# Chunk attention and two feed-forward layers on one core: where the scores of a group stand on TensorE, and in which array quadrants and banks

## The chip, the core and the metric

The kernel runs on one core of a Trainium2 chip. A core has TensorE (PE in the profile, PEld its weight loads), VectorE (DVE), ScalarE (ACT), GpSimd (POOL) and SyncE (SP), which here issues all the loads and stores. The metric is the device time of one execution in microseconds; lower is better.

## What is computed

Attention within chunks of 64 tokens (8 batches, 8 heads, 576 tokens, 64 features of a head), then two feed-forward layers over 4608 tokens of 512 features with 2048 hidden ones:

```python
def _attn_ref(q, k, v):            # chunk = 64, scale = 1 / sqrt(64)
    scores = scale * np.matmul(q_c, k_c.transpose(0, 1, 2, 4, 3))
    scores = scores - np.max(scores, axis=-1, keepdims=True)
    attn = np.exp(scores)
    attn = attn / (np.sum(attn, axis=-1, keepdims=True) + 1e-09)
    out = np.matmul(attn, v_c)

def _moe_ref(x, w_in, w_out):
    h = x @ w_in
    g = h * (1.0 / (1.0 + np.exp(-1.702 * h)))
    return g @ w_out

def _moe2_ref(x, w_in, w_out, alpha):
    h = x @ w_in
    g = np.maximum(h, 0.0) + alpha * np.minimum(h, 0.0)
    return g @ w_out
```

The weights come as 64-bit numbers and are decoded on the chip.

## The kernel before, in words

**Slots.** The first layer is a hand-written loop over 144 slots, n = 0 to 143: nine blocks of 512 tokens, in each of them the 16 slices of 128 hidden features. A slot issues on TensorE the 12 products H(n) (tile psH, line 454) and then the 12 products Y(n-2) (tile psY, line 476). ScalarE applies the activation to psH (line 461) and copies the result to the rounded part of gs (line 121); VectorE, in block 0 GpSimd, takes the rest (line 124). Two banks hold psH, four hold psY, two are left for the attention. At the end of a block psY is copied out (lines 487, 489), and the next block's x is split (`split_x`, lines 432 and 434). The second layer follows with other code; it is not changed.

**Engines keep the order of the program text.** The whole kernel is under one manual schedule: each engine, and SP's queue, takes its instructions in the order in which the Python code issues them. What fixes the order of the attention is the dictionary `between`, which hangs functions on half slots. An even place 2n is `middle` of slot n: behind the activation of H(n), ahead of the copy to gs and ahead of the decoding of weights. An odd place 2n+1 is the end of slot n, behind Y(n-2) and ahead of the slot's weight loads and preparation steps.

**Groups.** Attention goes by 36 groups g of 128 tokens (two chunks, all eight heads). Groups 0 to 3 and the scores of group 4 are done ahead of the loop, by the list `FIRST`. Group g from 5 on has its base at half slot 8(g-4), four slots a group, and goes through these steps:

- `att_T`, base-4: transposes q and k to qT and kT; by TensorE for groups up to 5 (line 318), by one VectorE instruction each from group 6 on (line 325).
- `att_S`, base-1: scores (psS, line 341), 16 float32 products of 64x64x64, each of which shows as two instructions in the trace. Product (head pair, chunk c, head j) reads rows j of the array and writes partitions j, all in one bank. Then VectorE's maximum (line 350) and subtraction (line 355) into e.
- `att_E`, base-1, directly behind: exponential on ScalarE (line 362), sum, addition and reciprocal on VectorE (lines 364 to 366), product on GpSimd (line 367). The exponential and the activation of h need different function tables, so a table load stands ahead of either when they change.
- `att_AT`, base+2: transposes e to `at`; for groups up to 7 by four TensorE transposes (line 383) and a ScalarE copy (line 388), from group 8 on by 16 VectorE transposes of 32x128 (line 393).
- `att_PV`, base+5: the sums (psX, line 410), again 16 products of 64x64x64, but product (head pair, c, j) reads rows c and writes partitions j of bank c. Two ScalarE copies (line 418) put them into x.
- `load_v` of the next group at base+6, and the q and k loads of the group after next in eight parts from base-1 to base+6 (line 300).

In block 0 each slot also decodes two slices of weights on VectorE (lines 156 to 171), which ScalarE and GpSimd then split (lines 121, 124). Slots 18 to 122 prepare the second layer's weights in 32 steps, each with such a decode whose first step on ScalarE (line 153) waits for its load.

A tile for psT, psS, psAT or half of psX is taken from the pool `ps_a`, two banks in turn, by `psum_att`.

Of the kernel before, what the change touches and what calls it, by code (L numbers as in the profile page):

```python
# [9 lines left out]
F32 = mybir.dt.float32  # L10
# [7 lines left out]
SQ = 32  # L18
# [31 lines left out]
def tile_chunk_attention_two_ffn(  # L50
# [45 lines left out]
    PS = bass.MemoryType.PSUM  # L96
    ps_y = banks.enter_context(tc.tile_pool(name="ps_y", bufs=4, space=PS, reuse_waits="tile"))
    ps_h = banks.enter_context(tc.tile_pool(name="ps_h", bufs=2, space=PS, reuse_waits="tile"))
    ps_a = banks.enter_context(tc.tile_pool(name="ps_a", bufs=2, space=PS, reuse_waits="tile"))

    ident = const.tile([P, P], F32, name="ident")
    alpha_sb = const.tile([P, NF], F32, name="alpha_sb")
# [8 lines left out]
    def psum_att(name):  # L111

        if ps_turn:
            pool, tag = ps_turn[0]
            ps_turn.append(ps_turn.pop(0))
            return pool.tile([P, 512], F32, tag=tag, name=name)
        return ps_a.tile([P, 512], F32, tag="a", name=name)

    def split(src, hi, lo, eng_hi, eng_lo):
        if eng_hi is nc.scalar:  # L120
# [236 lines left out]
        )  # L357
        e_t[g] = e

    def att_E(g):  # L360
        e = e_t[g]
        nc.scalar.activation(out=e, in_=e, func=AF.Exp, scale=SCALE)
        d = st_p.tile([P, 2 * HP, 1], F32, tag="d", name="d")
        nc.vector.reduce_sum(d, e, axis=AX.X)
        nc.vector.tensor_scalar_add(d, d, 1e-9)
        nc.vector.reciprocal(d, d)  # L366
        nc.gpsimd.tensor_tensor(  # L367
            out=e, in0=e, in1=d.to_broadcast([P, 2 * HP, CH]), op=ALU.mult
        )

    at_t = {}

    def att_AT(g):
        e = e_t.pop(g)
        if g < GPB:
            t = spare(f"wi{NF - GPB - 1 - g % 2}", 1).rearrange("p (h t) -> p h t", h=HP)
        else:
            t = at_p.tile([P, HP, P], F32, tag="at", name="at")

        if g < 2 * GPB:  # L380
            ps = psum_att("psAT")
            for hp in range(HP):
                nc.tensor.transpose(
                    ps[:, hp * P:(hp + 1) * P],
                    e[:, 2 * hp:2 * hp + 2, :].rearrange("p u t -> p (u t)"),
                    ident,
                )
            nc.scalar.copy(t.rearrange("p h t -> p (h t)"), ps)
        else:
            blocks = e.rearrange("p (h c) (b e) -> p h c b e", c=2, e=SQ)  # L390
            for i in range(P // SQ):
                for o in range(P // SQ):
                    nc.vector.transpose(  # L393
                        t[o * SQ:(o + 1) * SQ, :, i * SQ:(i + 1) * SQ],
                        blocks[i * SQ:(i + 1) * SQ, :, o // 2, o % 2, :],
                    )
        at_t[g] = t

    x_t = {}
# [1 line left out]
    def att_PV(g):  # L401
        at, vt = at_t.pop(g), qkv.pop((g, "v"))
        blk, i = divmod(g, GPB)
        if i == 0:
            x_t[blk] = x_p.tile([P, KT, NB], F32, tag="x", name="x")
        ps = [psum_att("psX") for _ in range(2)]
        for hp in range(HP):
            for c in range(2):
                for j in range(2):
                    nc.tensor.matmul(  # L410
                        ps[c][j * CH:(j + 1) * CH, hp * CH:(hp + 1) * CH],
                        vt[c * CH:(c + 1) * CH, 2 * hp + j, :],
                        at[c * CH:(c + 1) * CH, hp, j * CH:(j + 1) * CH],
                        start=True,
                        stop=True,
                    )
        for c in range(2):
            nc.scalar.copy(
                x_t[blk][:, :, i * P + c * CH:i * P + (c + 1) * CH],
                ps[c][:, :HP * CH].rearrange("p (h t) -> p h t", h=HP),  # L420
            )


    xs_t = {}
# [449 lines left out]
    with tc.manual_schedule():  # L874
# [28 lines left out]
            steps[step[:-1]](int(step[-1]))  # L903
        x_t.pop(0)
        ps_turn.clear()


        todo = {}
# [24 lines left out]

        between = {}
        for g in range(GPB, NG):
            for at, fn in zip((-4, -1, -1, 2, 5), (att_T, att_S, att_E, att_AT, att_PV)):
                if g > GPB or at > 0:
                    between.setdefault(8 * (g - GPB) + at, []).append((fn, g))
            if g + 1 < NG:
# [89 lines left out]
```

## Time and profile before

| | |
|---|---|
| median of 3 runs | 1633.4 us (1631.62 to 1634.8) |
| the profiled execution | 1633.03 us, of which 1631.1 us are the span of the profile |
| granted TensorE clock, mean | 0.993 of full |
| TensorE busy | 1586.6 us, 97% |
| weight loads | 1332.8 us, 82% |
| VectorE busy | 1121.7 us, 69% |
| ScalarE busy | 836.2 us, 51% |
| GpSimd busy | 487.6 us, 30% |
| attention products in the slots, psS / psX | 36.7 us / 23.3 us, 1024 instructions each |

All times count from the start of the span. Busy shares are means over stages with different limits, so the stretches are read one by one. In a row of the order of time the first number is the start and the second the length, both in us; an `xN` merges N instructions of one kind that stand behind each other, and the bracket at the end is the idle time of the engine just before, with what ended it.

### The profile page before, as it was taken

The page shows a single profiled execution, that of the slowest core. Times are in us where ns is not written, and L with a number is a line of the kernel's source. Part 1 is how long each engine was busy: PE and PEld are TensorE (multiplying, and loading weights), DVE is VectorE, ACT ScalarE, POOL GpSimd, SP SyncE. Part 2 cuts the span into 40 slices and gives each one's busy share as a digit, 9 for nine tenths or more (in the row PEclk, how much of TensorE's full clock was granted, in tenths as well). Part 3 has the DMA queues.
Part 4 walks back from the last instruction along what each step waited for, and adds up shares of the span by engine and source line. Part 5 has one row for each costly group of instructions (what it writes and reads, how often), then busy time and mean ns, then how long its engine had stood idle before and what let it go on. Part 6 is the DMA issues. An engine that isn't in the chain of part 4 may idle for free.

```text
span 1631.1 us, 25435 instructions
## 1 busy us (share of the span) xinstructions
PE 1586.6 (97%) x9257; PEld 1332.8 (82%) x9259; DVE 1121.7 (69%) x1634; ACT 836.2 (51%) x1198; POOL 487.6 (30%) x382
## 2 busy tenths in 40 slices
PE   6988999999999999999999999999999999999997
PEld 4766888888888888888888778888888888999997
DVE  7999566566566657657532267886788688778767
ACT  5555354444444544445433465566565556656653
POOL 3554122223132222222220034423523342342330
PEclk9999999999999999999999999999999999999999
DMA  9741444544453544444230457669767966997974
GB/s 243 209 133 22 97 114 110 128 111 123 107 137 95 141 121 111 121 121 131 68 136 0 169 171 244 199 188 245 249 190 206 269 197 211 227 343 244 257 262 124
DMA packets 384044, 268.07 MB, mean 164 GB/s; under 512 B 264112, under 2 KB 321968, under 8 KB 383920
## 3 DMA queue, kind: packets, MB, share of 16 engines
q1 hardware_dynamic: 383920, 266.46, 57.6%
q8 instruction: 73, 1.20, 0.3%
q14 instruction: 51, 0.42, 0.1%
HBM read 218.11 MB, written 48.23 MB: 163 GB/s over the span
## 4 chain that ended last, share of the span: by engine, by line
PE 88%; DVE 5%; DMA 2%; SPq 2%; issue 2%; ACT 1%; POOL 0%; DVEq 0%; POOLq 0%
PE psH L454 22%; PE psY L476 22%; PE psYa L773 12%; PE psHa L655 11%; PE psYb L773 9%; PE psHb L655 8%; PE psS L341 2%; DVE u L166 1%; PE psX L410 1%; SPq L277 1%; DVE u L156 1%; DVE u L171 1%; DMA wi2t<-wi 1%; DMA k<-in_k_dram 1%; DVE o L720 0%
## 5 line engine op out<-in xcount | busy, mean ns | idle before, releaser
L454 PE MATMUL psH<-xs,wi 128*128 128x512 f32 x1728 | 426.1, 397 | 5.2 <-DVE xs L123 5.2
L476 PE MATMUL psY<-gs,wo 128*128 128x512 f32 x1728 | 416.5, 391 | 0.0
L454 PEld LDWEIGHTS psH<-xs,wi 128*128 128x128 f32 x1728 | 322.0, 189 | 75.2 <-DVE xs L123 5.7
L476 PEld LDWEIGHTS psY<-gs,wo 128*128 128x128 f32 x1728 | 326.1, 189 | 67.8
L124 DVE TENSOR_TENSOR gs<-g,gs 128x512 fp32r<-128x512 f32 x129 | 95.2, 738 | 179.6 <-ACT gs L121 178.7
L773 PE MATMUL psYa<-o,w 128*128 128x512 f32 (+1 forms) x960 | 212.3, 369 | 4.8 <-DVE o L720 2.5
L655 PE MATMUL psHa<-xop,wi2t 128*128 128x512 f32 (+1 forms) x960 | 211.5, 369 | 3.0 <-DVE g L701 1.7
L773 PEld LDWEIGHTS psYa<-o,w 128*128 128x128 f32 x960 | 174.9, 188 | 29.8 <-DVE o L720 4.5
L655 PEld LDWEIGHTS psHa<-xop,wi2t 128*128 128x128 f32 x960 | 175.1, 188 | 27.6 <-DVE g L701 2.5
L461 ACT ACTIVATE g<-psH 128x512 f32<-128x512 f32 x144 | 86.2, 598 | 209.8 <-PE psH L454 209.0
L773 PE MATMUL psYb<-o,w 128*128 128x512 f32 (+1 forms) x720 | 158.4, 368 | 0.7 <-ACT o L715 0.7
L655 PE MATMUL psHb<-xop,wi2t 128*128 128x512 f32 (+1 forms) x720 | 158.3, 368 | 0.5 <-DVE g L701 0.5
L725 POOL TENSOR_TENSOR tsum<-g,tsum 128x1024 f32<-128x1024 f32 (+1 forms) x39 | 99.9, 2561 | 162.2 <-DVE o L720 162.2
L725 POOL TENSOR_TENSOR tsum<-g,g 128x1024 f32<-128x1024 f32 (+1 forms) x19 | 42.8, 2252 | 350.2 <-DVE g L678 344.5
L773 PEld LDWEIGHTS psYb<-o,w 128*128 128x128 f32 x720 | 131.3, 188 | 18.4 <-ACT o L715 1.3
L655 PEld LDWEIGHTS psHb<-xop,wi2t 128*128 128x128 f32 x720 | 131.4, 188 | 18.3 <-DVE g L701 0.9
L670 ACT ACTIVATE neg<-g 128x1024 f32<-128x1024 f32 (+1 forms) x80 | 78.1, 976 | 128.6 <-DVE g L701 128.0
L393 DVE STREAM_TRANSPOSE at<-e 32x128 f32<-32x128 f32 x448 | 135.5, 302 | 6.7
L367 POOL TENSOR_TENSOR e<-e,d 128x512 f32<-128x512 f32 x32 | 33.5, 1047 | 319.9 <-DVE d L366 275.5
L678 DVE SCALAR_TENSOR_TENSOR g<-g,neg 128x1024 f32<-128x1024 f32 (+1 forms) x80 | 104.5, 1306 | 19.4 <-ACT neg L672 19.4
L672 ACT ACTIVATE neg<-neg,minus_alpha 128x512 f32<-128x512 f32 (+1 forms) x160 | 100.2, 674 | 2.6
L720 DVE TENSOR_TENSOR o<-g,o 128x1024 fp32r<-128x1024 f32 (+1 forms) x60 | 96.3, 1605 | 5.5 <-ACT o L715 5.5
(111 smaller groups left out, 1828.5 us busy)
## 6 DMA issues: line engine op xcount, KB each, us to landing
wi2t<-wi SPq DMA_DIRECT2D x280, 256.0 KB, 3.7
w<-wo SPq DMA_DIRECT2D x140, 512.0 KB, 4.0
x<-ysb SPq DMA_DIRECT2D x36, 256.0 KB, 2.5
raw<-in_moe_w_in_dram SPq DMA_DIRECT2D x16, 512.0 KB, 5.1
raw<-in_moe_w_out_dram SPq DMA_DIRECT2D x16, 512.0 KB, 4.1
raw<-in_moe_w_in_dram SPq DMA_DIRECT2D x32, 256.0 KB, 3.9
wi<-stb SPq DMA_DIRECT2D x16, 512.0 KB, 3.0
raw<-in_moe_w_out_dram SPq DMA_DIRECT2D x32, 256.0 KB, 3.8
```

What stands on the lines that cost most here:

```text
L124: eng_lo.tensor_tensor(out=lo, in0=src, in1=hi.bitcast(F32), op=ALU.subtract)
L393: nc.vector.transpose(t[o * SQ:(o + 1) * SQ, :, i * SQ:(i + 1) * SQ], blocks[i * SQ:(i + 1) * SQ, :, o // 2, o % 2, :],)
L454: nc.tensor.matmul(ps, w[:, a, c], xs[:, b, c], start=(i == 0), stop=(i == 3 * KT - 1))
L461: nc.scalar.activation(out=g, in_=ps, func=AF.Gelu_apprx_sigmoid)
L476: nc.tensor.matmul(y_t[j][t], w[:, a, t * P:(t + 1) * P], gs[:, b], start=(f == 0 and a + b == 0), stop=(f == NF - 1 and b == 1),)
L655: nc.tensor.matmul(ps, w[:, c, a], x[b][:, c], start=(k == 0 and i in (1, 2, 5)), stop=(k == 5 and i in (2, 3, 4)), skip_group_check=True,)
L670: nc.scalar.activation(out=neg, in_=src, func=AF.Relu, scale=-1.0)
L672: nc.scalar.activation(out=neg[:, jj], in_=neg[:, jj], func=AF.Copy, scale=minus_alpha[:, f + jj:f + jj + 1])
L678: nc.vector.scalar_tensor_tensor(out=g, in0=g, scalar=0.0, in1=neg, op0=ALU.max, op1=ALU.add)
L720: nc.vector.tensor_tensor(out=lo, in0=wide(homes[nm], n), in1=hi.bitcast(F32), op=ALU.subtract)
L725: eng.tensor_tensor(out=wide(homes[out], n), in0=wide(homes[x], n), in1=wide(homes[y], n), op=ALU.subtract,)
L773: nc.tensor.matmul(ps[:, d, :n], w[:, jj, d, a], x[b][:, jj], start=(k == 0 and i in (1, 5, 2)), stop=(k == 5 and i in (3, 2, 4)), skip_gr ...
```

## The change

- The pool `ps_a` is closed behind the groups ahead of the loop. In its place one tile of two banks, `both[0]`, lives through the rest of the first layer. `psum_att` returns its two banks in turn, and `att_PV` writes the first half of either bank.
- `att_S` is no longer called in the slots. `att_PV(g)` issues the scores of group g+1 (`att_S_matmuls`) directly behind its own products, ahead of the ScalarE copies. They go into the second half of the banks: product (head pair, c, j) reads rows j, writes partitions c, in bank j. Maximum and subtraction (`att_S_max`) stand behind the copies. So the scores of group g stand at base-3, where they stood at base-1.
- `att_T` goes from base-4 to base-5, the exponential (`att_X`) from base-1 to base-2, which is the middle of a slot; sum, reciprocal and division (`att_N`) stay at base-1.
- e now has the chunk in the partitions. So `att_AT` of groups 5 to 7 becomes 16 float32 products with the identity of 64x64 each, and from group 8 on 8 VectorE transposes of 32x256 in place of 16 of 32x128.

```diff
+    att_banks = ExitStack()
+    ps_a = att_banks.enter_context(tc.tile_pool(name="ps_a", bufs=2, space=PS, reuse_waits="tile"))
+    both, ps_pair = [], []
@@ psum_att
-        return ps_a.tile([P, 512], F32, tag="a", name=name)
+        ps_pair.append(ps_pair.pop(0))
+        return ps_pair[0]
@@
+    def att_S_matmuls(g):
+        qt, kt = qkT.pop((g, "q")), qkT.pop((g, "k"))
+        s_t[g] = s4 = both[0][:, :, HP * CH:].rearrange("p j (h t) -> p h j t", h=HP)
+        for hp in range(HP):
+            for c in range(2):
+                for j in range(2):
+                    r = slice(j * CH, (j + 1) * CH)
+                    nc.tensor.matmul(
+                        s4[c * CH:(c + 1) * CH, hp, j, :],
+                        qt[r, hp, c * CH:(c + 1) * CH],
+                        kt[r, hp, c * CH:(c + 1) * CH],
+                        start=True,
+                        stop=True,
+                    )
+    def att_S_max(g):
+        s4 = s_t.pop(g)
+        m = st_p.tile([P, HP, 2, 1], F32, tag="m", name="m")
+        nc.vector.reduce_max(m, s4, axis=AX.X)
+        e = e_p.tile([P, 2 * HP, CH], F32, tag="e", name="e")
+        nc.vector.tensor_tensor(
+            out=e.rearrange("p (h j) t -> p h j t", j=2), in0=s4,
+            in1=m.to_broadcast([P, HP, 2, CH]), op=ALU.subtract,
+        )
+        e_t[g] = e
@@ att_AT
-        if g < 2 * GPB:
+        if g > GPB:
+            if g < 2 * GPB:
+                ps = psum_att("psAT")
+                for u in range(2 * HP):
+                    for c in range(2):
+                        r = slice(c * CH, (c + 1) * CH)
+                        nc.tensor.matmul(
+                            ps[r, u * CH:(u + 1) * CH], e[r, u, :], ident[r, r], start=True, stop=True
+                        )
+                nc.scalar.copy(t.rearrange("p h t -> p (h t)"), ps)
+            else:
+                t3 = t.rearrange("p h (j t) -> p (h j) t", j=2)
+                for i in range(P // SQ):
+                    for b in range(CH // SQ):
+                        o = i // 2 * 2 + b
+                        nc.vector.transpose(
+                            t3[o * SQ:(o + 1) * SQ, :, i % 2 * SQ:(i % 2 + 1) * SQ],
+                            e[i * SQ:(i + 1) * SQ, :, b * SQ:(b + 1) * SQ],
+                        )
@@ att_PV
-        ps = [psum_att("psX") for _ in range(2)]
+        if ps_pair:
+            ps = [both[0][:, c] for c in range(2)]
+        else:
+            ps = [psum_att("psX") for _ in range(2)]
...
+        if ps_pair and g + 1 < NG:
+            att_S_matmuls(g + 1)
         for c in range(2):
             nc.scalar.copy(
...
+        if ps_pair and g + 1 < NG:
+            att_S_max(g + 1)
@@ behind the steps of FIRST
+        att_banks.close()
+        ps_b = banks.enter_context(tc.tile_pool(name="ps_b", bufs=1, space=PS))
+        both.append(ps_b.tile([P, 2, 512], F32, tag="aa", name="psX"))
+        ps_pair += [both[0][:, c] for c in range(2)]
@@
-            for at, fn in zip((-4, -1, -1, 2, 5), (att_T, att_S, att_E, att_AT, att_PV)):
+            for at, fn in zip((-5, -2, -1, 2, 5), (att_T, att_X, att_N, att_AT, att_PV)):
```

## Rows read from the trace of the kernel before

**Rows 1.** Busy time by stretch: stretch, length; PE, PEld, DVE, ACT, POOL; clock.

```profile
99.00:138.00 39.00, 27.49 (x169) 22.21 (x169) 37.40 (x50) 21.51 (x36) 19.71 (x15) 0.89 0.24 54
...
444.00:540.00 96.00, 96.00 (x656) 78.04 (x652) 60.90 (x136) 45.20 (x71) 24.82 (x34) 1.00 0.45 116
```

**Rows 2.** TensorE in order of time: start, length, line, tiles, shape, count.

```profile
378.20 2.88 PE L476 MATMUL psY<-gs,wo 128*128 128x512 f32 x12
...
383.64 2.88 PE L476 MATMUL psY<-gs,wo 128*128 128x512 f32 x12
386.45 0.69 PE L410 MATMUL psX<-at,v 64*64 64x64 f32 x32
...
389.93 2.88 PE L476 MATMUL psY<-gs,wo 128*128 128x512 f32 x12
392.74 1.15 PE L341 MATMUL psS<-kT,qT 64*64 64x64 f32 x32
...
396.68 2.88 PE L476 MATMUL psY<-gs,wo 128*128 128x512 f32 x12
```

**Rows 3.** TensorE ahead of the loop: scores, then sums of another group.

```profile
28.41 1.08 PE L341 MATMUL psS<-kT,qT 64*64 64x64 f32 x29 [0.83 <-ACT kT L323]
...
29.38 0.64 PE L410 MATMUL psX<-early 64*64 64x64 f32 x30
```

**Rows 4.** VectorE in block 0, in order of time.

```profile
86.56 0.66 DVE L325 STREAM_TRANSPOSE kT<-k 128x512 f32<-128x512 f32 x1
...
102.40 0.69 DVE L364 TENSOR_REDUCE d<-e 128x8 f32<-128x512 f32 x1 [0.70 <-ACT e L362]
...
149.46 0.66 DVE L325 STREAM_TRANSPOSE kT<-k 128x512 f32<-128x512 f32 x1
...
155.30 3.17 DVE L434 TENSOR_TENSOR xs<-x,xs 128x512 fp32r<-128x512 f32 x4 [0.54 <-ACT xs L432]
```

**Rows 5.** TensorE in block 0, in order of time.

```profile
82.93 0.69 PE L410 MATMUL psX<-at,v 64*64 64x64 f32 x32
...
104.77 1.12 PE L383 MATMUL psAT<-ident,e 128*128 128x128 f32 x4 [6.01 <-POOL e L367]
...
137.16 1.11 PE L383 MATMUL psAT<-ident,e 128*128 128x128 f32 x4 [5.74 <-POOL e L367]
137.93 3.94 PE L476 MATMUL psY<-gs,wo 128*128 128x512 f32 x12
...
147.25 0.69 PE L410 MATMUL psX<-at,v 64*64 64x64 f32 x32
...
157.34 3.02 PE L454 MATMUL psH<-xs,wi 128*128 128x512 f32 x12
```

**Rows 6.** Group 33 at the start of a block: VectorE and TensorE.

```profile
740.27 5.08 DVE L393 STREAM_TRANSPOSE at<-e 32x128 f32<-32x128 f32 x16
...
745.25 0.83 PE L410 MATMUL psX<-at,v 64*64 64x64 f32 x32
...
746.62 0.67 DVE L325 STREAM_TRANSPOSE kT<-k 128x512 f32<-128x512 f32 x1
```

**Rows 7.** Loads of k for group 26, its transposition, landing times in 555 to 575.

```profile
562.55 1.99 SPq L300 DMA_DIRECT2D k<-in_k_dram  x4
...
572.99 0.70 DVE L325 STREAM_TRANSPOSE qT<-q 128x512 f32<-128x512 f32 x1
...
DMA to landing us min/median/max: 1.7/1.9/3.5
```

**Rows 8.** ScalarE behind a weight load, and the sums that it copies.

```profile
362.53 0.69 PE L410 MATMUL psX<-at,v 64*64 64x64 f32 x32
...
366.53 0.67 ACT L153 ACTIVATE u<-raw 128x512 f32<-128x512 f32 x1 [5.36 <-DMA raw<-in_moe_w_in_dram]
367.10 0.62 ACT L418 COPY x<-psX 128x256 f32<-128x256 f32 x2
...
368.90 1.28 ACT L362 ACT_TABLE_LOAD   x1
```

More of the change, by code (lines that the diff above doesn't have):

```diff
@@ L98, in tile_chunk_attention_two_ffn @@
     ps_h = banks.enter_context(tc.tile_pool(name="ps_h", bufs=2, space=PS, reuse_waits="tile"))
-    ps_a = banks.enter_context(tc.tile_pool(name="ps_a", bufs=2, space=PS, reuse_waits="tile"))
+    att_banks = ExitStack()
+    ps_a = att_banks.enter_context(tc.tile_pool(name="ps_a", bufs=2, space=PS, reuse_waits="tile"))
+    both, ps_pair = [], []
     ident = const.tile([P, P], F32, name="ident")
@@ L358, in att_S, with att_X, att_N @@
         e_t[g] = e
-    def att_E(g):
+    s_t = {}
+    def att_S_matmuls(g):
[22 more added lines that the diff above has]
+        e_t[g] = e
+    def att_X(g):
+        nc.scalar.activation(out=e_t[g], in_=e_t[g], func=AF.Exp, scale=SCALE)
+    def att_N(g):
         e = e_t[g]
-        nc.scalar.activation(out=e, in_=e, func=AF.Exp, scale=SCALE)
         d = st_p.tile([P, 2 * HP, 1], F32, tag="d", name="d")
@@ L369, in att_E @@
         )
+    def att_E(g):
+        att_X(g)
+        att_N(g)
     at_t = {}
@@ L388, in att_AT @@
             nc.scalar.copy(t.rearrange("p h t -> p (h t)"), ps)
[L389 to L396, printed above, removed]
         at_t[g] = t
@@ L405, in att_PV @@
             x_t[blk] = x_p.tile([P, KT, NB], F32, tag="x", name="x")
-        ps = [psum_att("psX") for _ in range(2)]
+        if ps_pair:
+            ps = [both[0][:, c] for c in range(2)]
+        else:
+            ps = [psum_att("psX") for _ in range(2)]
         for hp in range(HP):
```

## The prediction, made before the change was run

> **What bounds the kernel now.** I read the busy shares of stretches first, then TensorE's order of time, then the waits of the other engines. The reader is to see two stages inside the first layer. In block 0 (slots 0 to 15, up to about 157 us) VectorE decodes weights without a pause: from 99 to 138 us it is busy 37.40 of 39 us and TensorE only 27.49 [rows 1]. In the seven blocks after that TensorE is busy 96.00 of 96 us at full granted clock and VectorE 60.90 [rows 1]. So in block 0 a shorter TensorE step is worth nothing unless VectorE's chain gets shorter too, while from slot 16 on each TensorE microsecond that goes comes off the end. The second layer is not touched.
>
> **What one group costs TensorE.** Take the starts of psY [rows 2]. A plain slot (H, then Y) lasts 383.64 - 378.20 = 5.44 us. A slot that also holds the sums (psX) lasts 389.93 - 383.64 = 6.29, so the sums cost 0.85. A slot that holds the scores (psS) lasts 396.68 - 389.93 = 6.75, so the scores cost 1.31. Both are 32 instructions; the scores take 1.15 from first start to last end and the sums 0.69 [rows 2]. The scores of before use two quadrants, hence 16 rounds of two; the sums use four, hence 8 rounds of four. The difference of 8 rounds is 0.46 us, so 8 rounds cost 0.46.
>
> **Scores in four quadrants behind the sums.** New cost of the scores: their own 8 rounds, 0.46 us, with no entry and no exit of their own, since the sums before them have paid for both. That two different tiles follow each other without a seam is shown early in the trace, where scores started at 28.41 and the sums of another group came right behind: alone the scores end at 28.41 + 1.15 = 29.56, the sums ended at 29.38 + 0.64 = 30.02, 0.46 later [rows 3]. Each group saves 1.31 - 0.46 = 0.85. Bounds: the sums' pace is the fastest row there is for such matmuls, so 0.46 is the lower end; the upper end is the pace of two quadrants, 0.92, which leaves 0.39. I take 0.46, because the new scores go through the same four quadrants and the same two banks as the sums. Groups 9 to 35 lie in the stage that TensorE bounds: 27 x 0.85 = 22.9 us.
>
> **Block 0, groups 5 to 8.** VectorE's queue sets the pace here. Its sum of exponentials waited 0.70 us for ScalarE's exponential directly behind the subtraction [rows 4], in groups 5, 6 and 7 alike. With the subtraction a slot earlier the exponential is long done, so VectorE's chain gets 3 x 0.70 = 2.1 us shorter, and the transposition of group 7's probabilities, which waited 5.74 us for GpSimd's division, starts at 137.16 - 2.1 = 135.1 [rows 5]. Against that stands the earlier place of the scores. They now need qT and kT when the sums end, and in block 0 VectorE delivers these late: for group 6 the sums start at 82.93 and kT ends at 86.56 + 0.66 = 87.2; for group 8 it is 147.25 against 149.46 + 0.66 = 150.1 [rows 4, 5]. So TensorE waits at the scores of groups 6 and 7 for 4 to 5 us, and arrives at the transpositions about 1 us early instead of 6: the wait moves, it isn't added. What group 5's own steps win or lose at the start of the block, with four slots of VectorE's queue still ahead, ends in the 6.01 us wait of group 6 [rows 5]. Exit of the block: transposition of group 7 in its new form (16 products in two quadrants, priced like the old scores, 1.31) from 135.1 to 136.4; Y to 139.2, at full clock instead of the 3.94 us after the long wait [rows 5]; H and Y to 144.6; sums to 145.3; the scores of group 8 wait for kT until 150.1 - 2.1 = 148.0 and end at 148.6; H and two Y (8.3) bring slot 16 to 156.9, against 157.34 before [rows 5]: 0.4 us gained. Bounds: VectorE's split of x, which ended at 155.30 + 3.17 = 158.5 [rows 4], comes only 2.1 - 1.4 = 0.7 earlier, since the maximum and subtraction of group 8 now stand before it; H needs it after two thirds of its 2.9 us, so at most 1.4 is gained. On the other side the 2.7 us wait may lower the clock again; the rows put that at 1.1 (3.94 against a plain 2.88 [rows 2, 5]) and I allow twice as much, so at most about 1.8 is lost.
>
> **VectorE in the other blocks.** Transpositions of q and k move half a slot ahead and scores a whole one, so the cover between them shrinks from one and a half slots to one. In the tightest group, 33, kT ends at 747.29 while the sums start at 745.25 and end their share 0.6 later: 1.4 us late [rows 6]. What takes that away: 8 transpositions in place of 16. One of 32x128 takes 5.08 / 16 = 0.32 and one with four times the columns 0.67 [rows 6]; between them, an estimate of 0.44 for double the columns, 8 x 0.44 = 3.5 instead of 5.08, 1.5 us less in front of q and k. Also the maximum and subtraction (1.4 us) no longer stand in that stretch's queue. I leave 0.3 us for this one group; the six other groups at a block's start were late by under 1.0 and get the same relief, and the rest were ready in time.
>
> **Edits at no cost, and their cover.** The q and k loads keep their places on SP's queue, ahead of the value load as before. Transpositions come 2.7 us earlier; the shortest distance from the last k issue to the transposition is 572.99 - 564.54 = 8.4 us, landing takes at most 3.5 [rows 7], so 2.2 us are left. The exponential now stands between the activation of h and its split: one table load, 1.28 us [rows 8], and 0.6 of work, with the copy to gs behind it. That gs is read two slots later, some 11 us. The number of table loads stays. GpSimd's division keeps its place; its input is ready earlier.
>
> The lasting pair adds an order: sums and scores share both banks, so ScalarE's copies of the sums wait for the scores (0.46 later) and VectorE's maximum waits for the copies (0.62 more). Behind the copies stands the next activation, which waits for H, 2.9 us later; behind the maximum the prep's decode and the next split. The Trainium skill, "PSUM — Partial Sum Buffer", section Terms, speaks against sharing: two engines at one bank and quadrant at once are an error, reads against reads included. No run here shows that; by it the order can't be dropped, and rival (d) below keeps its mechanism; without it (d) would have no chance at all.
>
> **Sum.** 22.9 + 0.4 - 0.3 = 23.0 us. The profiled execution took 1633.03 us (span 1631.1), 0.4 under the median of three, 1633.4. That gives 1610.0 by the profiled one; I forecast 1610.
>
> **Rivals.**
> (a) The scores stand waiting for kT at each block's start, because the shorter transposition doesn't help as much as I think. Price: the 1.4 us of rows 6, seven times, 10 us: 1620. For it: TensorE itself gets 3.5% faster, which VectorE must follow. Against: VectorE has 35% to spare there [rows 1]. 9%.
> (b) Four quadrants run at the pace of two because the order of rows differs from the sums'. 27 x 0.39 = 10.5 us: 1622. Against: old scores alternated the same way. 5%.
> (c) Each small matmul has a floor of issue, so that 32 scores cost more than 8 rounds. Bounded by rows 2 between 0.46 and 0.92, at the middle 27 x 0.62 = 16.7: 1616. The Trainium skill, "TensorEngine Tiling (Array Packing)", section Performance Considerations, Instruction Overhead, states about 60 cycles for each matmul; an estimate by that page at 2.4 GHz is 32 x 25 ns = 0.8 us, or 1619. The sums' 32 within 0.69 us, the last one's own length included, say no [rows 2]. 3%.
> (d) Slower. Where ScalarE sits behind a weight load, as from 362.5 on, the sums' copies come at 367.10, 4.6 us after the sums' start [rows 8]. VectorE's maximum now waits for them, and its queue with it. Should this use up the distance from a split to the product that reads it (about two slots), TensorE waits some 4.6 us and loses 1.1 of clock, 5.7 a time. Four groups had such late copies (rows 8 stand for them), and 4 x 5.7 = 22.8 would eat the gain; from the fifth on the kernel is slower than before, and with six it stands at 1610 + 34 = 1644. Against: the decode behind the maximum waits for that same load anyway. 5%.
> (e) Block 0 gives more than 1.4 us: 1606 to 1608. 3%.
>
> **Chances.** Forecast (1606 to 1614) 75%, rivals as above. The range runs from 1606 to 1620: block 0 by its bounds (-1.4 to +1.8), the noise of the runs (1631.62 to 1634.8), and rivals (a) and (c); left out are (b) and (d). A measurement here tells 0.2% (3.3 us) from no change: faster 0.92, same 0.03, slower 0.05.
>
> **What would show it.** Right: psX and psS as one block of 64 in about 1.15 us; four slots with a group in 23.1 instead of 23.9 us; psY starts at full clock, no TensorE waits after slot 16; 8 transpositions in about 3.5 us; the sum of exponentials without its 0.70. Waits at psS for VectorE in groups 6 to 8, and short ones at psAT. Wrong: a seam or a gap inside psX and psS, waits at psS in later blocks, psY waiting for gs, or VectorE idle at the maximum with a queue behind it.

## The result, and the profile after

The changed kernel takes 1605.85 us (median; 1604.85 to 1607.76), the kernel before 1632.51 (median of 4; 1630.86 to 1634.8): a ratio of 0.9837, 95% interval 0.982 to 0.9854. The profiled execution took 1604.85 us, with a span of 1603.1 where before's was 1631.1. The time lies below the forecast of 1610 and just under the range, which began at 1606.

The 28.0 us of span lie here. H of slot 16, the end of block 0, starts at 152.61 in place of 157.34: 4.7 us. The seven blocks from there to the last one take 645.9 us in place of 668.7: 22.8 us. The last block takes 89.76 both times, and the second layer, whose code is the same, 0.5 less, which is not the change's. The forecast had 22.9 - 0.3 for the groups of the later blocks and 0.4 for block 0. So the term on which it rested came out, and block 0 gave more than the bound that I had put on it (1.4).

TensorE in order of time, after, around group 30 (start, length, line, tiles, shape, count):

```profile
671.25 2.88 PE L532 MATMUL psY<-gs,wo 128*128 128x512 f32 x12
674.06 0.69 PE L462 MATMUL psX<-at,v 64*64 64x64 f32 x32
674.57 0.65 PE L373 MATMUL psX<-kT,qT 64*64 64x64 f32 x32
675.15 3.02 PE L510 MATMUL psH<-xs,wi 128*128 128x512 f32 x12
678.01 2.88 PE L532 MATMUL psY<-gs,wo 128*128 128x512 f32 x12
```

The scores (line 373, named psX now since they share its tile) begin 0.51 us behind the first of the sums and end 1.16 behind it; the next H starts 1.09 behind the sums' start. The slot lasts 678.01 - 671.25 = 6.76 us, so sums and scores cost 6.76 - 5.44 = 1.32 together, where they cost 0.85 + 1.31 = 2.16 before [rows 2]. That is the 0.84 that the forecast put at 0.85, and four slots with a group last 23.08 us.

ScalarE and VectorE, after, behind the same products:

```profile
675.29 0.65 ACT L472 COPY x<-psX 128x256 f32<-128x256 f32 x2 [2.59 <-PE psX L373]
675.97 0.69 DVE L384 TENSOR_REDUCE m<-psX 128x8 f32<-128x512 f32 x1 [2.54 <-ACT x L472]
...
681.90 0.68 DVE L398 TENSOR_REDUCE d<-e 128x8 f32<-128x512 f32 x1
```

The order through the shared banks is there as foretold: the copies wait for the scores, the maximum for the copies. The sum of exponentials has no wait any more, where it had 0.70 [rows 4]. Over the whole kernel the maximum waits 69.4 us in 27 waits, and none of it reaches TensorE.

Busy time in the two stretches of [rows 1], after (us; PE, PEld, DVE, ACT, POOL, granted clock, DMA share, GB/s):

```profile
99.00:138.00 39.00, 33.18 (x250) 27.09 (x250) 38.86 (x49) 21.68 (x37) 23.54 (x18) 0.91 0.31 77
444.00:540.00 96.00, 96.00 (x685) 78.89 (x676) 57.45 (x107) 45.94 (x75) 25.43 (x34) 1.00 0.48 124
```

The later blocks are still TensorE's alone, at full clock. In block 0 VectorE is now busy 38.86 of 39 us; the wait for the exponential is gone from its queue, and TensorE is busy 5.7 us more in that stretch than before.

TensorE in block 0, after; a bracket is the idle time just before, with what ended it:

```profile
82.63 0.69 PE L462 MATMUL psX<-at,v 64*64 64x64 f32 x32
84.51 0.69 PE L373 MATMUL psX<-kT,qT 64*64 64x64 f32 x32 [1.19 <-DVE kT L328]
...
100.15 1.15 PE L424 MATMUL psX<-ident,e 64*64 64x64 f32 x32 [1.12 <-POOL e L401]
...
115.04 1.13 PE L373 MATMUL psX<-kT,qT 64*64 64x64 f32 x32 [4.70 <-DVE kT L328]
116.10 4.34 PE L510 MATMUL psH<-xs,wi 128*128 128x512 f32 x12
...
131.25 1.15 PE L424 MATMUL psX<-ident,e 64*64 64x64 f32 x32
...
143.65 0.69 PE L373 MATMUL psX<-kT,qT 64*64 64x64 f32 x32 [2.24 <-DVE kT L328]
144.27 3.06 PE L510 MATMUL psH<-xs,wi 128*128 128x512 f32 x12
...
152.61 2.88 PE L510 MATMUL psH<-xs,wi 128*128 128x512 f32 x12
```

The waits of 6.01 and 5.74 us at the transpositions of the probabilities [rows 5] are gone or 1.12 long, and three waits for kT stand at the scores. But everything is earlier than the forecast had it: the transposition for group 7 at 131.25 and not 135.1, the scores of group 8 at 143.65 and not 148.0.

### The profile page after: what moved, and what is told of

Its sections match the earlier page's. It is cut to its first block, busy times and chain, and to the rows that moved or that the text cites. A ratio compares the mean times of both kernels' runs of the same rounds, so it can differ in the third digit from the quotient of the medians.

```text
span 1603.1 us, 25410 instructions
## 1 busy us (share of the span) xinstructions
PE 1560.8 (97%) x9341; PEld 1318.4 (82%) x9343; DVE 1080.9 (67%) x1410; ACT 832.8 (52%) x1198; POOL 491.3 (31%) x382
## 4 chain that ended last, share of the span: by engine, by line
PE 88%; DVE 6%; issue 2%; SPq 1%; DMA 1%; ACT 1%; POOL 0%; DVEq 0%; POOLq 0%; ACTq 0%
PE psH L510 23%; PE psY L532 22%; PE psYa L829 12%; PE psHa L711 12%; PE psYb L829 9%; PE psHb L711 8%; DVE u L169 2%; PE psX L462 1%; DVE u L159 1%; SPq L280 1%; DVE u L174 1%; PE psX L373 1%; DMA wi2t<-wi 1%; DVE u L164 0%; DMA k<-in_k_dram 0%
## 5 line engine op out<-in xcount | busy, mean ns | idle before, releaser
L776 DVE TENSOR_TENSOR o<-g,o 128x1024 fp32r<-128x1024 f32 (+1 forms) x60 | 96.3, 1606 | 5.5 <-ACT o L771 5.5
L433 DVE STREAM_TRANSPOSE at<-e 32x256 f32<-32x256 f32 x224 | 97.5, 435 | 3.2
```

The costliest lines, as they stand in the source:

```text
L433: nc.vector.transpose(t3[o * SQ:(o + 1) * SQ, :, i % 2 * SQ:(i % 2 + 1) * SQ], e[i * SQ:(i + 1) * SQ, :, b * SQ:(b + 1) * SQ],)
L776: nc.vector.tensor_tensor(out=lo, in0=wide(homes[nm], n), in1=hi.bitcast(F32), op=ALU.subtract)
```

## What stood between the forecast and block 0

VectorE decodes two slices of weights a slot in block 0, in eight steps. Between the first H and the kT of group 8 that makes 109 steps in either kernel. A step takes 0.41 us (lines 159 and 164 after, 156 and 161 before) or 0.68 (169 and 174; 166 and 171) when nothing else runs. Many take about a microsecond more. VectorE and GpSimd of before, around group 5:

```profile
60.85 1.85 DVE L156 TENSOR_SCALAR u<-u 128x512 f32<-128x512 f32 x2
62.62 1.86 DVE L161 TENSOR_SCALAR u<-u 128x512 int32<-128x512 int32 x2
...
67.88 0.67 DVE L350 TENSOR_REDUCE m<-psS 128x8 f32<-128x512 f32 x1
...
61.05 1.36 POOL L124 TENSOR_TENSOR wo<-u,wo 128x512 fp32r<-128x512 f32 x1 [1.88 <-ACT wo L121]
62.37 1.49 POOL L124 TENSOR_TENSOR wi<-u,wi 128x512 fp32r<-128x512 f32 x1
```

and of after, at the same place:

```profile
60.61 0.68 DVE L384 TENSOR_REDUCE m<-psX 128x8 f32<-128x512 f32 x1
61.32 0.69 DVE L386 TENSOR_TENSOR e<-psX,m 128x512 f32<-128x512 f32 x1
61.93 1.90 DVE L159 TENSOR_SCALAR u<-u 128x512 f32<-128x512 f32 x2
63.75 0.75 DVE L164 TENSOR_SCALAR u<-u 128x512 int32<-128x512 int32 x2
...
67.54 0.56 DVE L399 TENSOR_SCALAR d<-d 128x8 f32<-128x8 f32 x1
...
60.82 1.29 POOL L127 TENSOR_TENSOR wo<-u,wo 128x512 fp32r<-128x512 f32 x1 [1.28 <-ACT wo L124]
62.07 1.48 POOL L127 TENSOR_TENSOR wi<-u,wi 128x512 fp32r<-128x512 f32 x1
66.72 1.35 POOL L127 TENSOR_TENSOR gs<-g,gs 128x512 fp32r<-128x512 f32 x1 [3.17 <-issue]
```

Before, each of the two GpSimd subtractions has a decode step of VectorE beside it, and each pair of steps takes 1.85 in place of 0.75: one step in each is stretched by 1.1 us. After, the first subtraction falls beside VectorE's maximum and subtraction, and these take their usual 0.68 and 0.69; only the second stretches a step. The small addition at 67.54 takes 0.56 beside the end of another GpSimd instruction, and 0.17 elsewhere. The reduction and the subtraction out of PSUM, the transpositions of q and k (0.66 and 0.70 with GpSimd beside them or not) and the sum are not stretched.

How far a step is stretched is not fixed. Each of the stretched steps up to kT, in before as in after, ends 0.28 to 0.29 us (the steps of 0.41) or 0.55 (those of 0.68) behind the end of a GpSimd instruction that began before it. So VectorE's step is held for as long as GpSimd's instruction still runs.

The accounts of VectorE from the first H to the end of kT of group 8 (lengths added up; steps that follow each other overlap by some 0.07 us): before 112.62 us, of which the decode takes 107.16 (45 steps stretched by over 0.2 us, 48.0 in all) and waits 2.09. After 106.33, with 102.89 in the decode (41 steps, 43.5) and no wait. So the path got 6.3 us shorter: the 2.1 that the forecast took away, and 4.3 that it had not thought of.

The Trainium skill, "SBUF — State Buffer", section Who interferes with whom, says that VectorE and GpSimd share one pair of SBUF ports, and that a VectorE instruction contends with GpSimd when it runs in a two-port mode, or when it has two inputs in SBUF and GpSimd's instruction reads SBUF, others not. The trace agrees in which instructions stretch: lines 169 and 174 read two tiles and 159 and 164 are the kind with such a mode, the maximum and the subtraction read PSUM; what a collision costs VectorE, about 1.07 us here (48.0 / 45 in before), is from these rows.

## The experiments

The theory: the pace and the missing seam carry the blocks, and in block 0 the collisions of decode steps with GpSimd, with the waits, set the end. The figures of all kernels, each from its profiled execution; "kT" is the end of kT of group 8, "stretched" counts decode steps up to it, "idle" is VectorE's waiting up to it, "block" the usual distance from one block's first H to the next in the blocks 1 to 6. The first H itself starts anywhere between 36.2 and 37.5, and the unchanged second layer takes 714.7 to 717.6, so places and blocks are compared, and the whole times only beside them. Each ratio is to runs of before made in the same set.

| kernel | kT | stretched | idle | slot 16 | block | median us (lowest to highest) | ratio to before |
|---|---|---|---|---|---|---|---|
| before | 150.12 | 45 | 2.1 | 157.34 | 95.68 | 1632.51 | |
| after | 143.59 | 41 | 0 | 152.61 | 92.32 | 1605.85 | 0.9837 |
| e1_two_quadrants | 143.59 | 41 | 0 | 152.89 | 93.55 | 1614.89 (1614.56 to 1616.74) | 0.989 (0.9875 to 0.9905) |
| e2_own_place | 147.00 | 38 | 7.9 | 153.12 | 93.87 | 1618.14 (1616.64 to 1621.33) | 0.9912 (0.989 to 0.9933) |
| e3_late_maximum | 148.92 | 42 | 4.4 | 159.49 | 92.32 | 1613.6 (1612.79 to 1614.41) | 0.988 (0.9857 to 0.9903) |
| e4_mid_decode | 145.81 | 43 | 0 | 154.79 | 92.32 | 1609.69 (1609.51 to 1609.87) | 0.9856 (0.9834 to 0.9878) |
| e5_more_gpsimd | 149.72 | 49 | 0 | 158.69 | 92.32 | 1612.06 (1611.83 to 1612.29) | 0.9871 (0.9851 to 0.9892) |
| e6_late_transposes | 145.37 | 42 | 2.1 | 154.38 | 92.32 | 1607.83 (1606.59 to 1608.47) | 0.9845 (0.983 to 0.9859) |
| e7_sixteen_transposes | 143.27 | 41 | 0 | 152.24 | 92.32 | 1606.44 (1606.41 to 1606.47) | 0.9839 (0.9819 to 0.9858) |
| e8_gs_on_vector | 138.31 | 26 | 2.6 | 147.33 | 92.32 | 1599.23 (1598.44 to 1601.49) | 0.9795 (0.978 to 0.981) |
| e9_all_on_vector | 131.99 | 4 | 3.1 | 140.96 | 92.32 | 1595.29 (1593.75 to 1595.97) | 0.9767 (0.9751 to 0.9784) |
| e10_before_on_vector | 131.07 | 4 | 2.9 | 141.00 | 95.68 | 1617.68 (1616.8 to 1619.28) | 0.991 (0.9893 to 0.9926) |

**The pace of four quadrants.** The same products in an order in which only two quadrants can work at a time:

```diff
-        for hp in range(HP):
-            for c in range(2):
-                for j in range(2):
+        for d in range(2):
+            for hp in range(HP):
+                for c in range(2):
+                    j = c ^ d
```

> Kernel after with the scores in the same place, banks and layout, but issued so that only two of the four quadrants alternate (first the pairs of equal chunk and head parity, then the others). Theory (the scores cost 8 rounds of four, 0.46 us): 16 rounds of two cost 0.92, so 0.46 more a group, a block of four groups 92.32 + 1.84 = 94.2 us, the kernel 27 x 0.46 = 12.4 us longer than after, about 1618; block 0 unchanged (slot 16 starts at 152.6 to 153.1). Rival (the quadrants bring nothing, only the missing seam does): a block stays at 92.3 and the time at 1606.

TensorE in this kernel:

```profile
681.09 0.69 PE L463 MATMUL psX<-at,v 64*64 64x64 f32 x32
681.60 0.94 PE L374 MATMUL psX<-kT,qT 64*64 64x64 f32 x32
682.47 3.03 PE L511 MATMUL psH<-xs,wi 128*128 128x512 f32 x12
```

The scores take 0.94 us in place of 0.65 and H comes 0.87 behind their start in place of 0.58; a block is 1.23 us longer, 0.31 a group. The order of the rows does set the pace, but not by the full 0.46. A likely reason, which no run shows, is that the two halves of the products overlap where they meet. The kernel is 9.0 us longer than after (12.4 was expected), and slot 16 stays at 152.89, as expected.

**The seam.** Scores in four quadrants, but at the place that they had before, each with an entry and an exit of its own:

```diff
-            for at, fn in zip((-5, -2, -1, 2, 5), (att_T, att_X, att_N, att_AT, att_PV)):
+            for at, fn in zip((-4, -1, -1, 2, 5), (att_T, att_S4, att_E, att_AT, att_PV)):
```

`att_S4` is `att_S_matmuls` and `att_S_max` behind each other.

> Kernel after with the scores in four quadrants and the lasting pair, but in their old place at the end of the slot ahead of the base, with maximum, exponential and division there as before. Theory: the scores get entry and exit of their own, 0.39 us, and cost 0.85 like the sums, so a block of four groups takes 95.68 - 4 x 0.46 = 93.8 us. Block 0 goes back towards the kernel before, as the maximum stands behind a decode again: slot 16 starts at 156 to 158. In all 27 x 0.39 + 4.5 = 15 us over after, about 1621. Rival (standing behind the sums is what counts, by more than the seam): a block near 95.7, the time near 1630.

TensorE in this kernel:

```profile
689.51 0.69 PE L373 MATMUL psX<-kT,qT 64*64 64x64 f32 x32
690.13 3.02 PE L510 MATMUL psH<-xs,wi 128*128 128x512 f32 x12
```

The scores alone look like the sums, 0.69 us long. A block takes 93.87: 1.81 less than before, 0.45 a group for the quadrants, and 1.55 more than after, 0.39 a group for the seam. So the 0.84 splits into 0.45 and 0.39. Slot 16 was expected at 156 to 158 and came at 153.12, and the kernel is at 1618.14 in place of 1621. VectorE waits 7.9 us here, yet its path from the first H to kT is 1.8 us shorter than in the kernel before (110.8 against 112.6): while VectorE waits, GpSimd gets its instructions done beside nobody, and only 38 steps are stretched. And with the scores a whole slot behind kT, slot 16 follows kT by 6.1 us and not by 9.0. A wait of VectorE in block 0 is therefore not lost in full.

**Where the maximum stands.** In groups 5 to 8 alone, maximum, subtraction and exponential go back to the old place (base-1), behind the decode:

```diff
-        if ps_pair and g + 1 < NG:
+        if ps_pair and g + 1 < NG and g + 1 > 2 * GPB:
             att_S_max(g + 1)
@@ the loop that fills `between`
+                if GPB < g <= 2 * GPB and fn is att_X:
+                    continue
+                if GPB < g <= 2 * GPB and fn is att_N:
+                    between.setdefault(8 * (g - GPB) - 1, []).extend([(att_S_max, g), (att_X, g)])
```

> Kernel after, but for groups 5 to 8, in block 0, the maximum, the subtraction and the exponential stand at the old place, a slot later, with the sum directly behind; the scores stay behind the sums of the group before. Theory (the maximum's place on VectorE is what made block 0 shorter: 2.1 us of waiting for the exponential, and some 4 us because GpSimd's splits then fall on maximum and subtraction, which they don't stretch, instead of on decode steps, which they do): slot 16 starts at 152.6 + 2.1 + 4.2 - 1.4 = 157.5, give or take 1; kT of group 8 ends at 149 to 150 instead of 143.6; the number of stretched decode steps goes back from 38 to 42. Rival (TensorE's shorter steps and smaller waits in block 0 made it shorter): slot 16 stays within 1 us of 152.6.

VectorE in this kernel:

```profile
97.52 0.69 DVE L386 TENSOR_TENSOR e<-psX,m 128x512 f32<-128x512 f32 x1
101.22 0.69 DVE L398 TENSOR_REDUCE d<-e 128x8 f32<-128x512 f32 x1 [3.01 <-ACT e L393]
```

kT came at 148.92 and slot 16 at 159.49 (157.5, give or take 1, was expected), 5.3 and 6.9 us behind after, so the block's gain hangs on where these steps stand. But 4.4 of the 5.3 us at kT are waits for the exponential, one of them 3.01 long, and only one more step is stretched than the 41 of after (not the 38 that the expectation starts from). This kernel takes back the gain by the other term, and doesn't tell the two apart.

**The collisions without the wait.** Maximum, subtraction and exponential in the middle of the decode instead, between its second and third pair of steps, so that the sum has its exponential in time:

```diff
                 op0=ALU.logical_shift_left, op1=ALU.bitwise_and,
             )
+        yield
         for u, hi in zip(us, his):
@@ slot loop
+                if (2 * n + 2) % 8 == 0 and GPB < g <= 2 * GPB:
+                    next(dec)
+                    att_S_max(g)
+                    att_X(g)
                 for _ in dec:
```

Here g is the group whose base is at half slot 2n + 2; at their new place the three steps are skipped for groups 5 to 8, by lines not shown.

> Kernel after, but for groups 5 to 8 maximum and subtraction stand between the two halves of the next decode, some 4 us later on VectorE, and the exponential behind them. The exponential is still done ahead of the sum, so the 0.70 us waits stay away; but GpSimd's two weight splits, which start when the decode before ends, now fall on decode steps alone. Theory (GpSimd's overlap accounts for about 4.2 us): kT of group 8 ends 3 to 4.5 us later than in after, at 146.6 to 148.1, and slot 16 starts at 155.5 to 157. Rival (the waits alone, or TensorE, made block 0 shorter): kT of group 8 stays at 143.6 and slot 16 at 152.6.

VectorE in this kernel, around group 5:

```profile
61.49 2.95 DVE L164 TENSOR_SCALAR u<-u 128x512 int32<-128x512 int32 x2
64.36 0.68 DVE L385 TENSOR_REDUCE m<-psX 128x8 f32<-128x512 f32 x1
```

VectorE never waits here, and still kT is 2.2 us later than in after: 43 steps are stretched in place of 41, and the decode takes 104.97 us in place of 102.89, 2.1 more. The rows show one such place: two shift steps take 2.95 us beside GpSimd's two subtractions (those of after, at 63.75, took 0.75), and the maximum comes when GpSimd has nothing to do. So a maximum that isn't beside GpSimd costs by collisions alone, but half of the 4.3 us that lie between before and after. kT (145.81) and slot 16 (154.79) came ahead of the expected 146.6 to 148.1 and 155.5 to 157.

**One more GpSimd instruction a slot.** In slots 2 to 8 GpSimd adds a spare 128x512 tile to itself; nobody waits for it:

```diff
+            if 2 <= n <= 8:
+                more = spare("wo15", 1)
+                nc.gpsimd.tensor_tensor(out=more, in0=more, in1=more, op=ALU.add)
```

> Kernel after with seven more GpSimd instructions in block 0, one at the start of each of slots 2 to 8, an addition of 128x512 to a tile that nothing reads any more; nothing waits for them but GpSimd itself. Theory (a GpSimd instruction that overlaps a decode step on VectorE stretches that step by about 1.07 us, the difference between 43.5 and 48.0 us of excess over 41 and 45 stretched steps): 6 or 7 more stretched steps, VectorE's path to kT of group 8 6 to 7.5 us longer (143.6 to about 150 to 151), slot 16 at 158 to 160, the kernel 5.5 to 7 us longer than after, about 1612. Rival (the two engines don't touch each other and the steps are long for a reason of their own): nothing changes but GpSimd's busy time; kT at 143.6.

Seven instructions of 1.22 us bring eight more stretched steps, and kT is 6.1 us later, 0.88 for each, with no wait of VectorE (the expectation's 1.07 is 48.0 / 45, not the difference that it names). Slot 16 moves by the same 6.1. The end of block 0 goes with the number of GpSimd instructions, although no engine waits for the added ones.

**Fewer of them.** First GpSimd's remainder of gs goes to VectorE, 14 instructions up to kT; then the remainders of the weights too, behind the second pair of decode steps, 28 more:

```diff
-            emit_h(n, middle, nc.gpsimd if ("decode", n) in todo else nc.vector)
+            emit_h(n, middle, nc.vector)
@@ in the second of the two only
-        split(dec_t.pop((kind, l, f)), t[:, 0], t[:, 1], nc.scalar, nc.gpsimd)
+            src = dec_t.pop((kind, l, f))
+            nc.scalar.copy(t[:, 0], src)
+            later.append((t[:, 1], src, t[:, 0].bitcast(F32)))
...
+                next(dec, None)
+                while lows:
+                    lo, whole, hi = lows.pop(0)
+                    nc.vector.tensor_tensor(out=lo, in0=whole, in1=hi, op=ALU.subtract)
```

> Kernel after with the remainder of gs in block 0 on VectorE in place of GpSimd (13 instructions). Theory (a GpSimd instruction costs VectorE about 1.07 us where it meets a decode step, and the same work on VectorE costs it 0.69): VectorE's path to kT of group 8 gets some 13 x (1.07 - 0.69) = 5 us shorter, slot 16 starts 3 to 5 us sooner, about 149, and the kernel is at 1601 to 1603. Rival (moving work onto the engine that sets the pace makes it slower): slot 16 some 9 us later, about 161, the kernel at 1614.

> As the kernel with gs on VectorE, and the remainders of the weights too (28 instructions), between the halves of the next decode, so that GpSimd keeps only the division in block 0. Theory: 41 instructions at 0.69 on VectorE in place of 41 stretches of 1.07, some 15 us less on VectorE's path; it then no longer sets the pace, TensorE does, whose waits in block 0 after slot 2 add up to 9 us with 1.5 of lost clock: slot 16 at 143 to 147, the kernel at 1596 to 1600. Rival (more work on VectorE makes it slower): slot 16 after 165.

VectorE by line in block 0 up to kT (busy us, mean ns of one | idle before): first after, then the second of the two.

```profile
L164 DVE TENSOR_SCALAR u<-u 128x512 int32<-128x512 int32 x27 | 26.5, 1020 | 0.0
L169 DVE SCALAR_TENSOR_TENSOR u<-raw,u 128x512 int32<-128x512 int32 x27 | 24.8, 957 | 0.0
L159 DVE TENSOR_SCALAR u<-u 128x512 f32<-128x512 f32 x28 | 24.8, 924 | 0.0
L174 DVE SCALAR_TENSOR_TENSOR u<-raw,u 128x512 int32<-128x512 int32 x27 | 22.6, 876 | 0.0
```

```profile
L175 DVE SCALAR_TENSOR_TENSOR u<-raw,u 128x512 int32<-128x512 int32 x27 | 17.4, 682 | 0.0
L170 DVE SCALAR_TENSOR_TENSOR u<-raw,u 128x512 int32<-128x512 int32 x27 | 17.4, 682 | 0.0
L159 DVE TENSOR_SCALAR u<-u 128x512 f32<-128x512 f32 x28 | 13.8, 531 | 0.0
L164 DVE TENSOR_SCALAR u<-u 128x512 int32<-128x512 int32 x27 | 10.2, 417 | 0.0
L127 DVE TENSOR_TENSOR gs<-g,gs 128x512 fp32r<-128x512 f32 x14 | 9.6, 683 | 1.1 <-ACT gs L124 1.1
```

VectorE does more work and is done sooner. With gs alone kT comes 5.3 us earlier, with all remainders 11.6: the decode falls from 102.9 us to 62.9 (lengths added up, the rows leave overlaps out), and the 42 remainders that VectorE takes over cost 0.68 each, 28.6. Four stretched steps are left, as many as GpSimd keeps divisions. Slot 16 starts at 140.96, earlier than the 143 to 147 expected, and the kernel takes 1595.29 us (ratio to before 0.9767, interval 0.9751 to 0.9784), just under the expected 1596 to 1600; with gs alone it takes 1599.23, where 1601 to 1603 was expected. TensorE has one wait of over half a microsecond left in the second half of block 0, 0.52 at 107.00.

The hold seems to go the other way at times. With gs alone on VectorE, one GpSimd remainder, usually 1.3 to 1.6 us long, lasts 5.38, while the eight decode steps beside it run at their short lengths (first GpSimd, then two of VectorE's rows); e3_late_maximum has one of 4.76 at 93.27:

```profile
52.41 5.38 POOL L127 TENSOR_TENSOR wo<-u,wo 128x512 fp32r<-128x512 f32 x1 [3.48 <-ACT wo L124]
...
53.48 0.75 DVE L164 TENSOR_SCALAR u<-u 128x512 int32<-128x512 int32 x2
54.15 1.28 DVE L169 SCALAR_TENSOR_TENSOR u<-raw,u 128x512 int32<-128x512 int32 x2
```

No run shows what decides which of the two is held.

**The same in the kernel before.** The remainders go to VectorE in the kernel before the change, by the same edit:

> Kernel before, with the remainders of block 0 on VectorE as in the kernel that has all of them there. Theory (GpSimd's overlap is a cost of block 0 by itself, and the change won 4.3 us of its 28 by shifting it): slot 16 starts at 143 to 148 instead of 157.3, blocks stay at 95.68, the kernel at 1619 to 1624; against it the change then brings the blocks' 23 us and, where TensorE sets the pace in block 0 too, the same 0.84 a group there: 24 to 27 us to 1595. Rival (only with the maximum a slot earlier does this help): slot 16 at 152 or later.

TensorE, the first H of slot 16 (a part of its 12 products), first in this kernel, then in after with the same edit:

```profile
141.00 1.19 PE L460 MATMUL psH<-xs,wi 128*128 128x512 f32 x4
```

```profile
140.96 1.30 PE L516 MATMUL psH<-xs,wi 128*128 128x512 f32 x5
```

With four collisions left in either, both kernels reach slot 16 at the same time (counted from the first H, after is 0.8 us sooner), and the change brings 22.1 us of span, 1615.4 to 1593.3: 23.0 in the seven blocks, less 0.9 by which the unchanged second layer took longer. So what block 0 gained by the change, 4.7 us, came all but 0.8 from collisions and waits on VectorE, and is not there to gain where these are gone. Two expectations missed: this kernel was put at 143 to 148 for slot 16 and 1619 to 1624 us and came at 141.00 and 1617.68, and the 0.84 a group that block 0 was to give too did not come.

**The earlier transpositions, and the wider ones.** The forecast gave two reasons why q and k would be ready for the earlier scores. First, the transpositions go back to base-4, with the scores where they are now:

```diff
-            for at, fn in zip((-5, -2, -1, 2, 5), (att_T, att_X, att_N, att_AT, att_PV)):
+            for at, fn in zip((-4, -2, -1, 2, 5), (att_T, att_X, att_N, att_AT, att_PV)):
```

> Kernel after with the transposition of q and k at its old place, half a slot later, while the scores stay behind the sums: half a slot of cover in place of one. Theory of the prediction (the cover counts at the start of each block): the transposition then stands behind the preparation's decode and the next slot's start, TensorE waits at the scores for kT in most groups at a block's start, by 1 to 3 us each, so 7 to 20 us over all and about 1615 to 1625. Rival (VectorE has enough room there): waits at the scores in block 0 alone, and at most 2 us over after.

Blocks stay at 92.32, the scores wait for kT in block 0 alone, and the kernel is 2.0 us over after, nearly all of it by slot 16 (1.8 later). In group 33 kT ends 0.06 us ahead of the scores in either kernel, since in VectorE's queue the two places are the same there: the transposition of the probabilities and the remainder of gs stand ahead of q and k both times. In all other groups behind block 0 kT ends at least 1.27 us ahead. My theory of 7 to 20 us fell. Second, 16 transpositions in place of 8, in two halves each:

```diff
-                        nc.vector.transpose(
-                            t3[o * SQ:(o + 1) * SQ, :, i % 2 * SQ:(i % 2 + 1) * SQ],
-                            e[i * SQ:(i + 1) * SQ, :, b * SQ:(b + 1) * SQ],
-                        )
+                        for u in (slice(0, HP), slice(HP, 2 * HP)):
+                            nc.vector.transpose(
+                                t3[o * SQ:(o + 1) * SQ, u, i % 2 * SQ:(i % 2 + 1) * SQ],
+                                e[i * SQ:(i + 1) * SQ, u, b * SQ:(b + 1) * SQ],
+                            )
```

> Kernel after with the transposition of the probabilities in 16 instructions of 32x128 again in place of 8 of 32x256, same layout. Theory of the prediction (the shorter transposition is what brings kT in time at the start of a block): 5.1 us in place of 3.6 in front of q and k, TensorE waits at the scores of the groups at a block's start, up to 1.4 us each, a block of 92.32 becomes up to 93.7 and the kernel up to 10 us longer. Rival (room enough, as the late transposition of q and k showed): blocks at 92.32, no waits there, time as after, 1605 to 1607; block 0 the same, as groups 5 to 7 don't use it.

Group 33 at the start of block 7, first in after, then in this kernel:

```profile
715.24 3.60 DVE L433 STREAM_TRANSPOSE at<-e 32x256 f32<-32x256 f32 x8
...
720.85 0.69 PE L373 MATMUL psX<-kT,qT 64*64 64x64 f32 x32
```

```profile
715.08 4.06 DVE L434 STREAM_TRANSPOSE at<-e 32x128 f32<-32x128 f32 x16
...
721.13 0.69 PE L373 MATMUL psX<-kT,qT 64*64 64x64 f32 x32 [0.58 <-DVE kT L328]
```

The halves take 4.06 us, not the 5.08 of [rows 6], so this takes away only 0.46 of the 1.5 us of relief. That is enough for one wait of 0.58 us in group 33, and no other group waits: the last of the seven blocks takes 92.67 in place of 92.01, the rest are as they were. The tightest group thus has no slack at all, and each microsecond that the wider form saves is worth about one there, once; the six other groups at a block's start had room (kT ends at least 0.80 us ahead of the scores even here).

## Why the prediction was off, point by point

- **Four quadrants, no seam** (0.85 a group, 22.9 us): right, 0.84 and 22.8. Quadrants 0.45 and seam 0.39, as the reading of [rows 2, 3] had it. The price of rival (c) is refuted: 32 products cost 0.46 to 0.47 us behind the sums (1.09 us for both, against 0.62 from the start of a lone set to H in the second experiment). Rival (b) would have left 0.39 of the 0.85 a group; two quadrants at a time lost 0.31 in the first experiment and left 0.53.
- **Block 0** (0.4 us, bounds -1.8 to +1.4): wrong; it gave 4.7. The step that failed is "VectorE's chain gets 3 x 0.70 = 2.1 us shorter", which took the lengths of the decode steps as fixed. They depend on what GpSimd does at the same time: the chain got 6.3 shorter, kT of group 8 came at 143.59 and not at 148.0, and from there slot 16 followed after 9.0 us, as foretold (8.9), at 152.6 and not at 156.9. The upper bound fell with it: it said that the split of x comes only 0.7 us earlier, and it ended at 152.6 in place of 158.5, 5.9 earlier (row below). Rival (e) had the direction right, at 3%, but no mechanism, and even its 1606 was too high: the forecast's own sum with 4.7 for block 0 gives 1605.7.

```profile
150.12 2.49 DVE L490 TENSOR_TENSOR xs<-x,xs 128x512 fp32r<-128x512 f32 x4
```

- The rows that could have told stand in the trace of before, where pairs of steps of one line take 1.28 or 2.37 us (line 166), 1.83 or 2.95 (line 161). A bound taken from a chain whose steps vary by a factor of two has to price what makes them vary.
- **Waits in block 0**: they moved from the transpositions to the scores, as foretold; 1.19 and 4.70 us at groups 6 and 7 where 4 to 5 was expected at each, 2.24 at group 8 where 2.7 was.
- **The stall of group 33** (0.3): the scores start 0.63 behind the sums there and 0.51 elsewhere, 0.12 lost. The estimate for 8 transpositions (3.5) measured 3.59 to 3.60. The relief was needed as said; the earlier place of the transpositions was not, so rival (a) had less to stand on than I gave it. Of the 1.5 us of relief only 0.46 come from the wider form; the rest came with the new layout of e, which I had not counted (4.06 against 5.08 for the same 16).
- **Edits at no cost, and rival (d)**: the exponential, the table loads and the maximum behind the copies cost nothing that TensorE shows. There is no wait of TensorE in the blocks behind slot 16.
- What stays open: moving the maximum brought back two of the four collisions (2.1 of 4.3 us). The traces say where the four lie. In before all but three of GpSimd's 48 instructions stretch a decode step, in after all but seven; of the four more, three begin beside the maximum of groups 5, 6 and 7 (60.82, 90.68 and 121.16) and one beside the sum of group 5 (66.72). In e4_mid_decode none of them has the maximum at its start, but one falls beside a sum (129.85) and one lasts 2.37 beside short decode steps (124.20), so that run could bring back only two. No run brings back all four without adding waits of VectorE.

## What to carry to other kernels

Small matmuls in quadrants should stand together: here a set of 32 costs 0.46 us behind another set and 0.39 more where it enters and leaves the full array alone, and the order of quadrants must keep all four at work. Where VectorE bounds a stage and GpSimd "helps" it, compare the lengths of like VectorE instructions first; if they vary, price a move by which of them will meet a GpSimd instruction and how long that one is, and try giving the work back to VectorE (0.68 us there against 1.07 of stretch). And a wait removed from such a queue is worth neither its own length nor a fixed bound, since the other engine used it.

## What the chip showed that I had not expected

- A GpSimd instruction, here mostly of 1.2 to 1.5 us on 128x512 in SBUF, holds a decode step of VectorE until it ends, which costs about 1.07 us, nearly one step for each (48 instructions and 41 stretched steps up to kT in after, 5 and 4 with the remainders on VectorE). VectorE's maximum and subtraction out of PSUM, its sum and its transpositions keep their lengths beside it.
- TensorE's clock: in block 0 of after the wait of 4.70 us was followed by an H of 4.34 (granted clock 0.57 of full from 111 to 119 us, so the lower level, 1.2 GHz, for most of it); the wait of 2.24 us was followed by one of 3.06, at 2.4 GHz (1.00 from 143 to 150).
- Transpositions of the same 32x128 took 5.08 us for 16 in before [rows 6] and 4.06 when they read e in the layout of after. Nothing else about them differs that the trace shows.
